# Loading and transposing q and k by head pair in a fused attention and maxout-FFN kernel

## The chip, the cores and the metric

The kernel runs on one core of one Trainium2 chip. The metric is the device time of one execution in microseconds, as the median of five runs. The core's engines go by the names of the profile: PE multiplies matrices (PEld loads its weights), DVE and ACT do elementwise work, POOL and SP mostly issue DMAs here.

## The reference

Attention with a relative-position bias over 8 batches, 8 heads, 576 positions and 64 channels, and then a feed-forward network with the largest of three products as its gate:

```python
scores = scale * np.matmul(q, k.transpose(0, 1, 3, 2)) + bias      # q, k, v: (8, 8, 576, 64), float32
attn = np.exp(scores - np.max(scores, axis=-1, keepdims=True))
attn = attn / (np.sum(attn, axis=-1, keepdims=True) + 1e-09)
attn_out = np.matmul(attn, v)
x = attn_out.transpose(0, 2, 1, 3).reshape(B * S, H * D)           # 4608 tokens of 512
h = np.maximum(np.maximum(x @ w1, x @ w2), x @ w3)                 # d_ff = 768
out = h @ w_out
```

The bias depends on the distance of the two positions only, by 32 buckets.

## The kernel before

**Steps.** The two heads of a pair share the 128 partitions, so the work goes in steps (b, hp): batch b from 0 to 7, head pair hp from 0 to 3. A step multiplies kT by qT into PSUM (`sc`, and `sct` and `scq` for the last 64 positions, the tail), ACT takes the exponential into bf16 (`e`, `el`; line 808), DVE multiplies a band around the diagonal by the bias (line 788), and a later step multiplies with v (`a`) and divides (`x_sb`). The FFN of an earlier chunk of 512 tokens is woven into the steps: `ps` and `psp` are its gates, `pso` and some `psp` its output. PE's instructions are in an order written out by hand (`keep_in_program_order`), so one late operand holds all of PE.

**Where q and k come from.** `load_qk` loads, on POOL's queue, for each of four blocks of 128 positions all eight heads of q, then of k, into tiles `q_sb` and `k_sb` of shape [128, KT, H, D] (line 189), and casts from float32 to bf16 on the way; the tails go to `qtail` and `ktail` (lines 170 and 192). From batch 2 on, `transposes(b)` turns them on SP's queue by DMA, one instruction for a block of positions with all four head pairs, ten in a batch (line 719), into `qT` and `kT` of shape [128, HP, positions]. Batch 1 takes another way: its q and k come in a packed layout into space of `xT`, `spread_packed` copies a head pair into `q_sb` and `k_sb` on DVE (line 236; the first pair on POOL), and PE transposes it. Step (1, hp) has the copies for pair hp + 1 ahead of its FFN portion.

**Order of the loads.** POOL's queue holds, one behind the other: the first weights, the packed batch 1, v of batch 1, `moe_w3`; then q and k of batch 2, all of it; then in step (1, 2) v of batch 2 (lines 161 and 180), the output weights `wo_bf` (line 1065) and q and k of batch 3; and in step (b, 2) v of batch b + 1 and q and k of batch b + 2. `go_behind` makes some of these wait for transposes: `load_v` for a named kT transpose of the same batch, `load_last_weights` and the next q and k for the last one of main blocks. From batch 5 on (`PACED`) a load also waits for the one four places ahead (`DEEP`). The weights load whole (line 1046).

**SP's queue.** It holds the q and k transposes, the transposes of finished attention rows `x_sb` into `xT` (lines 954 and 1002, five in a batch, which the FFN gates read), and the stores of outputs (lines 450 and 564). It works in order: what waits at its head holds the rest.

**Buffers.** q and k tiles, `qT` and `kT`, `x_sb` and v have two each, output rows five. In step (3, 0) the scores run in another order (`keys_first`), with both halves of the queries for the first two key blocks ahead of the others.

Of the kernel before, what the change touches and what calls it, by code (L numbers as in the profile page):

```python
# [39 lines left out]
def kernel(  # L40
# [12 lines left out]
    nc = tc.nc  # L53
# [8 lines left out]
    QM = 2 * QS  # L62
    KT = 4
    ROWS = (4, 0)
    PACED, DEEP = 5, 4
    FCH = d_ff // P
    DCH = d_model // P
    NTOK = B * S
# [73 lines left out]
    def main_part(src, b):  # L142
        return src[b, :, 0 : KT * P, :].rearrange("h (t p) d -> p t h d", p=P)

    def tail_part(src, b, h0, h1, par):
        return src[b, h0 + par : h1 : 2, KT * P : S, :].rearrange("h p d -> p h d")

    in_flight = []

    def in_turn(b, load):  # L150
        load = inorder(load)
        if b >= PACED:
            if len(in_flight) >= DEEP:
                go_behind([load], in_flight[-DEEP])
            in_flight.append(load)
        return load

    def load_main(src, b, h0, h1, dst, t0=0, t1=KT):
        x = main_part(src, b)
        return [  # L160
            in_turn(b, nc.gpsimd.dma_start(out=dst[:, t, h0:h1, :], in_=x[:, t, h0:h1, :])) for t in range(t0, t1)  # L161
        ]
# [5 lines left out]
    def load_q_tail(b):  # L168
        dst = qtail[b % 2][0 : S - KT * P].rearrange("p g (h d) -> p (g h) d", h=2)
        return in_turn(b, nc.gpsimd.dma_start(out=dst, in_=q[b, :, KT * P : S, :].rearrange("h p d -> p h d")))  # L170

    def k_diag(b, par, h0, h1):
        return diag(ktail[b % 2], par, h0, h1)
# [7 lines left out]
            for par in range(2)  # L181
        ]

    def load_qk(b, behind=None):

        loads = []
        for t in range(KT):
            for src, dst in zip((q, k), batch[b]):
                loads.append(in_turn(b, nc.gpsimd.dma_start(out=dst[:, t], in_=main_part(src, b)[:, t])))  # L189
        loads.append(load_q_tail(b))  # L190
        for par in range(2):
            load = nc.gpsimd.dma_start(out=k_diag(b, par, 0, H), in_=tail_part(k, b, 0, H, par))
            loads.append(in_turn(b, load))
        go_behind(loads, behind)

    def go_behind(loads, behind):

        for load in loads if behind else ():
            tc.add_manual_dep(
                load.ins, behind.ins.name,  # L200
                mybir.DependencyInfo(mybir.DependencyClass.Sync, mybir.DependencyReason.DATA),
                reason="these loads go behind the transposes in line",
            )

    def load_v(b, h0, h1, behind=None):
        loads = load_main(v, b, h0, h1, vx[b % 2][:, :, :, 0:D]) + load_tail(v, b, h0, h1, v_diag)
        go_behind(loads, behind)
        return loads[-1]

# [23 lines left out]
        for dst, src in zip(batch[1], (q_1, k_1)):  # L235
            inorder(eng.tensor_copy(dst[:, :, h, :], src[:, h].rearrange("p h t d -> p t h d")))  # L236

    def load_tiles():
        q_sb = loads.tile([P, KT, H, D], BF16, tag="q_sb", name="q_sb")
        k_sb = loads.tile([P, KT, H, D], BF16, tag="k_sb", name="k_sb")  # L240
        return q_sb, k_sb

    batch = [None] * B
    batch[0] = load_tiles()
# [464 lines left out]
    def transposes(b):  # L709

        made = qk_tiles()
        qk.append(made)

        def one(j, t):
            n = P if t < KT or j else S - KT * P
            src = batch[b][j][:, t].rearrange("p h d -> p (h d)") if t < KT else (
                (qtail, ktail)[j][b % 2][0:n].rearrange("p h c -> p (h c)")
            )
            turned_qk[b, j, t] = inorder(nc.sync.dma_start_transpose(out=made[j][:, :, P * t : P * t + n], in_=src))  # L719

        for t in range(KT + 1):
            one(0, t)
            one(1, t)
            yield

    def qk_tiles():
        return [qkt.tile([P, HP, n], BF16, tag=x, name=x) for x, n in (("qT", S), ("kT", (KT + 1) * P))]
# [174 lines left out]
            out=last_tile, in0=last_tile, in1=hank[:, 2 * hp : 2 * hp + 2, P - 64 : P][:, :, ::-1], op=ALU.mult,  # L902
        ))

    divided, turned_qk = {}, {}

    def attend(b, hp, e4, el, half):

# [134 lines left out]

    def load_w(i):
        src = (moe_w1, moe_w2, moe_w3)[i].rearrange("(c p) f -> p c f", p=P)
        in_turn(0, nc.gpsimd.dma_start(out=w_bf[i][:], in_=src))

    load_w(0)
    batch[1] = load_tiles()
# [11 lines left out]
        load_v(1, 0, H)  # L1061
        load_w(2)

    def load_last_weights(behind):
        load = in_turn(0, nc.gpsimd.dma_start(out=wo_bf[:], in_=moe_w_out.rearrange("(c p) m -> p c m", p=P)))
        go_behind([load], behind)

    def bands(hp):
        times_band_pair(hp, first_e[hp], 0, 0)
# [42 lines left out]
    for hp in range(HP):  # L1112
        qT, kT = (x[:, hp, :] for x in qk[0])
        if begun:
            e4, el = begun.pop()
            more_transposes(hp + 1)
            scores(qT, kT, e4, 1, 2)
        else:
            e4, el = e_tiles()
            visit(qT, kT, e4, [(1, 0), (1, 2)], (lambda: more_transposes(hp + 1)) if hp + 1 < HP else None)  # L1120

        def keys():
            left_keys(hp, qT, kT, el, QS, S)

        def queries():
            left_queries(hp, qT, kT, el)

        def late_bands(hp=hp, e4=e4):
            times_band(hp, e4, 1, QS, QM, inorder)
            times_band_pair(hp, e4, 2, QS)  # L1130

        if hp == 0:
            keys()
        if hp == 1:
            x_transposes(0, 0)
        quotients = next_late()
        if hp < 2:
            if hp == 0:
                make_bandt()
            quotients()  # L1140
            if hp == 0:
                bands(2)
            else:
                behind.pop()()
                keys()
            queries()
            if hp == 1:
                x_transposes(1, 0)
            else:
                begun.append(e_tiles())  # L1150
                scores(*(x[:, 1, :] for x in qk[0]), begun[0][0], 1, 0)
            quotients = next_late()
            quotients()
            if hp == 0:
                bands(3)
            behind.append(lambda late_bands=late_bands, hp=hp, el=el: (late_bands(), products(hp, el)))
        else:
            if behind:
                behind.pop()()
            if hp == 3:  # L1160
                quotients()
                add_ffn(0, QS)
                fill(8)
            keys()
            if hp == 2:
                quotients()
            queries()
            late_bands()
            if hp == 2:
                x_transposes(2, 0)  # L1170
                x_transposes(3, 0)
            else:
                batch[2] = load_tiles()
                load_qk(2)
                x_transposes(0, 1)
                fill(8, lambda: second_transposes(qk[1], 0))
            products(hp, el)
        late.append(lambda hp=hp, e4=e4, el=el: attend(0, hp, e4, el, 1))

    turned = [lambda hp=hp: x_transposes(hp, 1) for hp in range(1, HP)]  # L1180
    for b, hp in [(b, hp) for b in range(1, B) for hp in range(HP)]:
# [15 lines left out]

        if tiled:
            run, after = stages.pop(0)
        keys_first = (b, hp) == (3, 0)  # L1200
        order = [(0, 0), (1, 0), (0, 2), (1, 2)] if keys_first else [(0, 0), (0, 2), (1, 0), (1, 2)]
        if rows:
            lead = not begun
            begun.clear()
# [6 lines left out]
            for c, tt in order[:2]:  # L1211
                scores(qT, kT, e4, c, tt)
        store_outputs()
        if b == 1:
            if hp == 0:
                crossbar = transposes(2)
            next(crossbar, None)
        elif hp and b + 1 < B:
            if hp == 1:
                crossbar = transposes(b + 1)  # L1220
            for _ in range((KT + 1, 2, KT + 1)[min(b, 4) - 2]):
                next(crossbar, None)
        early()
        if turned:
            turned.pop(0)()
# [4 lines left out]
        quotients()  # L1230
        if rows:
            times_band(hp, e4, 1, 0, QM, inorder)
        if b == 1 and hp + 1 < HP:
            spread_packed(hp + 1, nc.vector)
        if (b, hp) == (1, 1):
            add_ffn(QS, QS)

# [64 lines left out]
        else:  # L1302
            late_keys = (b, hp) == (2, 0)
            fill(8 if (b, hp) == (2, 1) else rate, (lambda: None) if late_keys else keys, *([lambda: None] if together else []))
            if not late_keys:
                times_bandt(hp, el)

# [5 lines left out]

            visit(qT, kT, e4, order[2:], None if together else beside_scores, el=el if together else None)
        store_outputs()
        if b == 1 or hp in (1, 2) and b + 1 < B:
            for _ in range(2 if b > 1 else 1):
                next(crossbar, None)
        early()
        if turned:  # L1320
            turned.pop(0)()
# [6 lines left out]
        if hp == 1 and b > 1:  # L1328
            pending.extend((n, [fn]) for n, fn in rest)
            rest.clear()  # L1330
            made, tail = ffn((b - 1) * CH, CH, False, [(b + (i + 2) // HP, (i + 2) % HP) >= ROWS for i in range(HP)])
        if hp == 2 and b + 1 < B:
            load_v(b + 1, 0, H, turned_qk[b + 1, 1, 1 if b < 3 else 2 if b == 3 else KT - 1])
            if b == 1:
                load_last_weights(turned_qk[2, 1, KT - 1])
                batch[3] = load_tiles()
                load_qk(3, turned_qk[2, 1, KT - 1])
        if hp == 2 and 1 < b < B - 2:
            batch[b + 2] = load_tiles()
            load_qk(b + 2, turned_qk[b + 1, 1, KT - 1])  # L1340

        def queries():
            times_band(hp, e4, 3, 0, QM, inorder)
# [70 lines left out]
```

## Time and profile before

| | |
|---|---|
| device time, median of 5 runs | 310.24 us (308.88 to 312.71) |
| the profiled execution: device time, span | 310.34 us, 308.6 us |
| PE, PEld | 297.1 us (96%), 181.9 us (59%) |
| DVE, ACT, POOL | 207.1 us (67%), 202.0 us (65%), 110.5 us (36%) |
| granted PE clock | 1.0 throughout |
| DMA packets | 163950, of which 153784 are under 512 B |
| HBM read, written | 35.39 MB, 9.45 MB |

The span runs from the first to the last instruction of the program; the device time holds 1.74 us more. Busy times are unions over an engine's instructions. In the lines of a view, "<-" in brackets names what ended the idle time ahead of an instruction, and an issue on POOL or SP is the time that the queue took to hand a transfer over, not the time to its landing.

### The profile page before, as it was taken

To read this page: it belongs to the slowest core of one execution; us is meant where nothing else is said; L and a number is where in the kernel's file an instruction comes from. 1 tells how busy PE (TensorE), PEld (TensorE's weight loads), DVE (VectorE), ACT (ScalarE), POOL (GpSimd) and SP (SyncE) were. 2 spreads that over 40 slices of the span, in tenths; PEclk is the share of its full clock that TensorE was granted. 3 is DMA by queue.
4 is the path that set the end of the run, shared out by engine and by line. 5 is a ranking of instruction groups with operands and counts; after the bars stand their busy time and mean duration, and the time that the engine had idled before them with its cause. 6 is when DMAs were issued, how large, how long until landed. Compare 5 with 4: busy or idle time off the path is not lost.

```text
span 308.6 us, 10546 instructions
## 1 busy us (share of the span) xinstructions
PE 297.1 (96%) x4547; PEld 181.9 (59%) x4547; DVE 207.1 (67%) x471; ACT 202.0 (65%) x273; POOL 110.5 (36%) x147
## 2 busy tenths in 40 slices
PE   7889989989999999999999999999999999999995
PEld 2367867765555655657666766666667654444442
DVE  7497878766776767666777677766777665553552
ACT  3999979976777777758777777777777730222211
POOL 8978650962096106630555145434100000000000
PEclk9999999999999999999999999999999999999999
DMA  9999999999999999999999979997922113202003
GB/s 158 191 199 198 181 165 143 95 166 142 165 135 225 135 199 144 130 135 155 173 106 159 163 138 161 126 174 165 135 53 107 37 19 94 102 0 104 34 0 136
DMA packets 163950, 40.48 MB, mean 131 GB/s; under 512 B 153784, under 2 KB 159424, under 8 KB 163904
## 3 DMA queue, kind: packets, MB, share of 16 engines
q0 software_dynamic: 103840, 16.66, 85.0%
q1 hardware_dynamic: 58304, 22.69, 42.1%
q8 instruction: 35, 0.57, 0.8%
q10 hardware_dynamic: 1760, 0.47, 0.7%
q14 instruction: 11, 0.09, 0.1%
HBM read 35.39 MB, written 9.45 MB: 145 GB/s over the span
## 4 chain that ended last, share of the span: by engine, by line
PE 84%; DMA 5%; ACT 5%; SPq 3%; issue 1%; DVE 1%; ACTq 0%; POOL 0%
PE psp L108 34%; PE ps L108 17%; PE a L108 12%; PE sc L108 8%; PE pso L108 6%; ACT e L808 4%; SPq L719 3%; DMA wo_bf<-in_moe_w_out_dram 3%; PE sct L108 2%; PE scq L108 1%; PE warm L108 1%; DMA qT<-qtail 1%; DMA out_dram<-osb 1%; PE tp L112 1%; PE xp L112 0%
## 5 line engine op out<-in xcount | busy, mean ns | idle before, releaser
L808 ACT ACTIVATE e<-sc 128x1024 bf16<-128x1024 f32 x128 | 128.6, 1026 | 31.6 <-PE sc L108 30.3
L108 PEld LDWEIGHTS <-w_bf 64*128 64x128 bf16 (+1 forms) x1088 | 73.6, 95 | 57.2 <-issue 2.7
L108 PE MATMUL psp<-xT,w_bf 64*128 64x512 bf16 x736 | 91.4, 376 | 0.7 <-issue 0.7
L788 DVE TENSOR_TENSOR e<-e,hank 128x512 bf16<-128x512 bf16 (+2 forms) x120 | 56.4, 475 | 17.6 <-ACT e L808 17.2
L108 PE MATMUL ps<-xT,w_bf 128*128 128x512 bf16 (+1 forms) x352 | 65.1, 335 | 0.8 <-DVE q_sb L236 0.8
L108 PE MATMUL sc<-qT,kT 64*128 64x256 bf16 (+1 forms) x384 | 47.7, 306 | 2.1 <-ACT e L808 1.0
L108 PEld LDWEIGHTS <-kT 64*128 64x128 bf16 (+1 forms) x736 | 30.5, 94 | 26.7 <-issue 9.5
L108 PE MATMUL a<-vx,e 64*128 64x65 bf16 (+1 forms) x1536 | 44.6, 191 | 0.0
L161 POOL DMA_DIRECT2D vx<-in_v_dram x28 | 24.6, 894 | 55.7 <-DMA kT<-k_sb 32.2
L108 PEld LDWEIGHTS <-e 64*128 64x128 bf16 (+1 forms) x1536 | 40.7, 95 | 3.8
L108 PEld LDWEIGHTS <-hT 64*128 64x128 bf16 (+1 forms) x444 | 27.3, 95 | 20.1 <-issue 1.4
L108 PE MATMUL a<-vt,el 64*128 64x65 bf16 (+1 forms) x240 | 30.8, 201 | 0.2 <-DVE m L496 0.2
L406 ACT ACTIVATE m<-ps 128x512 bf16<-128x512 f32 x14 | 8.4, 597 | 34.3 <-PE ps L108 34.3
L108 PEld LDWEIGHTS <-el 64*128 64x128 bf16 (+1 forms) x624 | 26.0, 95 | 7.8 <-issue 5.2
L808 ACT ACTIVATE el<-sct 128x576 bf16<-128x576 f32 (+2 forms) x36 | 21.7, 606 | 13.3 <-PE sct L108 12.1
L108 PE MATMUL psp<-wo_bf,hT 64*128 64x256 bf16 (+1 forms) x336 | 29.7, 307 | 0.0
L189 POOL DMA_DIRECT2D k_sb<-in_k_dram x24 | 21.5, 895 | 11.1 <-DMA k_sb<-in_k_dram 6.3
L189 POOL DMA_DIRECT2D q_sb<-in_q_dram x24 | 21.5, 898 | 9.3 <-DMA q_sb<-in_q_dram 5.7
L108 PE MATMUL pso<-wo_bf,hT 128*128 128x512 bf16 (+2 forms) x108 | 23.2, 367 | 0.8 <-DMA wo_bf<-in_moe_w_out_dram 0.8
L808 ACT ACTIVATE el<-scq 128x512 bf16<-128x512 f32 (+1 forms) x38 | 19.5, 530 | 2.8 <-PE scq L108 2.7
L415 DVE TENSOR_TENSOR m<-ps,m 128x512 bf16<-128x512 f32 x14 | 9.7, 692 | 17.0 <-PE ps L108 17.0
L536 DVE TENSOR_TENSOR hT<-psp,m 128x1024 bf16<-128x1024 f32 (+1 forms) x16 | 15.0, 956 | 7.4 <-PE psp L108 7.4
(83 smaller groups left out, 291.8 us busy)
## 6 DMA issues: line engine op xcount, KB each, us to landing
out_dram<-osb SPq DMA_DIRECT2D x35, 256.0 KB, 3.9
vx<-in_v_dram POOLq DMA_DIRECT2D x28, 128.0 KB, 6.6
q_sb<-in_q_dram POOLq DMA_DIRECT2D x26, 128.0 KB, 7.4
k_sb<-in_k_dram POOLq DMA_DIRECT2D x24, 128.0 KB, 7.9
w_bf<-in_moe_w_dram POOLq DMA_DIRECT2D x3, 768.0 KB, 9.3
xT<-in_k_dram SPq DMA_DIRECT2D x6, 128.0 KB, 4.5
hank<-w_dr SPq DMA_DIRECT2D x2, 384.0 KB, 5.4
wo_bf<-in_moe_w_out_dram POOLq DMA_DIRECT2D x1, 768.0 KB, 9.8
```

What stands on the lines that cost most here:

```text
L108: made = inorder(nc.tensor.matmul(*args, **kw))
L112: inorder(nc.tensor.transpose(*args))
L161: in_turn(b, nc.gpsimd.dma_start(out=dst[:, t, h0:h1, :], in_=x[:, t, h0:h1, :])) for t in range(t0, t1)
L189: loads.append(in_turn(b, nc.gpsimd.dma_start(out=dst[:, t], in_=main_part(src, b)[:, t])))
L406: nc.scalar.activation(out=st[fb]["m0"][:], in_=ps0, func=ACTF.Copy)
L415: inorder(nc.vector.tensor_tensor(out=m[:], in0=ps1, in1=st[fb]["m0"][:], op=ALU.max))
L536: inorder(nc.vector.tensor_tensor(out=out_[:, i : i + n], in0=ps2()[:, i : i + n], in1=m[0][:, i : i + n], op=ALU.max,))
L719: turned_qk[b, j, t] = inorder(nc.sync.dma_start_transpose(out=made[j][:, :, P * t : P * t + n], in_=src))
L788: put(nc.vector.tensor_tensor(out=e4[:, t, :, lo:hi], in0=e4[:, t, :, lo:hi], in1=hank[:, 2 * hp : 2 * hp + 2, c0:c1][:, :, ::-1], op=ALU. ...
L808: made = nc.scalar.activation(out=out_, in_=in_, func=ACTF.Exp, scale=inv_sqrt_d)
```

## The change

From batch 2 on q and k are loaded by head: `load_pair(b, g)` issues four loads for head pair g (q and k, even and odd head), each with all four blocks of positions, into tiles of shape [128, HP, KT, 2, D]. A transpose takes one head pair with its four blocks (line 725 of the changed file), another the tails (line 732); there are ten in a batch as before. `begin_qk` loads pair 0, the tails and pair 1; `end_qk` loads pairs 2 and 3, and stands behind v of the same batch and, for batch 2, the output weights. The transposes stand in SP's order at places written out by step and half step. The loads wait for no transposes any more. From step (1, 1) on each load, v included, waits for the sixth one ahead of it. `moe_w2` and `moe_w3` load in two pieces, the first 256 columns and the other 512. The copies of `spread_packed` come behind the FFN portion of their step, and `keys_first` is gone.

```diff
-    PACED, DEEP = 5, 4
+    DEEP = 6
...
-        if b >= PACED:
-            if len(in_flight) >= DEEP:
+        if b > 1:
+            if len(in_flight) >= DEEP and paced:
                 go_behind([load], in_flight[-DEEP])
             in_flight.append(load)
...
-    def load_qk(b, behind=None):
...
-        for t in range(KT):
-            for src, dst in zip((q, k), batch[b]):
-                loads.append(in_turn(b, nc.gpsimd.dma_start(out=dst[:, t], in_=main_part(src, b)[:, t])))
...
-        go_behind(loads, behind)
+    def load_pair(b, g):
+        for src, dst in zip((q, k), batch[b]):
+            for par in range(2):
+                part = main_part(src, b)[:, :, 2 * g + par, :]
+                in_turn(b, nc.gpsimd.dma_start(out=dst[:, g, :, par, :], in_=part))
...
+    def begin_qk(b):
+        batch[b] = load_tiles(True)
+        load_pair(b, 0)
+        load_left(b)
+        load_pair(b, 1)
+
+    def end_qk(b):
+        for g in range(2, HP):
+            load_pair(b, g)
...
+        def pair(g):
+            for j in range(2):
+                inorder(nc.sync.dma_start_transpose(
+                    out=made[j][:, g, 0 : KT * P].rearrange("p (t n) -> p t n", t=KT),
+                    in_=batch[b][j][:, g].rearrange("p t h d -> p (t h d)"),
+                ))
...
+        return [lambda: pair(0), left] + [lambda g=g: pair(g) for g in range(1, HP)]
...
-        in_turn(0, nc.gpsimd.dma_start(out=w_bf[i][:], in_=src))
+        for f0, f1 in ((0, QS), (QS, d_ff)) if i else ((0, d_ff),):
+            in_turn(0, nc.gpsimd.dma_start(out=w_bf[i][:, :, f0:f1], in_=src[:, :, f0:f1]))
...
+    places = {2: ((1, 1, 0), (1, 1, 1), (1, 2, 0), (1, 3, 1), (2, 1, 0)), 3: ((2, 2, 0), (2, 2, 1), (2, 3, 0), (3, 0, 0), (3, 0, 1))}
+    for n in range(4, B):
+        places[n] = tuple((n - 1, hp, half) for hp, half in ((1, 0), (1, 1), (2, 0), (2, 1), (3, 0)))
...
-        if hp == 2 and b + 1 < B:
-            load_v(b + 1, 0, H, turned_qk[b + 1, 1, 1 if b < 3 else 2 if b == 3 else KT - 1])
+        if hp == 1 and b + 1 < B:
+            paced.append(b)
+            load_v(b + 1, 0, H)
             if b == 1:
-                load_last_weights(turned_qk[2, 1, KT - 1])
-                batch[3] = load_tiles()
-                load_qk(3, turned_qk[2, 1, KT - 1])
-        if hp == 2 and 1 < b < B - 2:
-            batch[b + 2] = load_tiles()
-            load_qk(b + 2, turned_qk[b + 1, 1, KT - 1])
+                load_last_weights()
+            end_qk(b + 1)
+        if hp == (2 if b == 1 else 1) and b + 2 < B:
+            begin_qk(b + 2)
```

More of the change, by code (lines that the diff above doesn't have):

```diff
@@ L146, in tail_part @@
         return src[b, h0 + par : h1 : 2, KT * P : S, :].rearrange("h p d -> p h d")
-    in_flight = []
+    in_flight, paced = [], []
     def in_turn(b, load):
         load = inorder(load)
-        if b >= PACED:
-            if len(in_flight) >= DEEP:
+        if b > 1:
+            if len(in_flight) >= DEEP and paced:
                 go_behind([load], in_flight[-DEEP])
@@ L182, in load_tail, with load_left @@
         ]
-    def load_qk(b, behind=None):
-        loads = []
-        for t in range(KT):
-            for src, dst in zip((q, k), batch[b]):
-                loads.append(in_turn(b, nc.gpsimd.dma_start(out=dst[:, t], in_=main_part(src, b)[:, t])))
[L190 to L193, printed above, removed]
-        go_behind(loads, behind)
+    def load_pair(b, g):
[3 more added lines that the diff above has]
+                in_turn(b, nc.gpsimd.dma_start(out=dst[:, g, :, par, :], in_=part))
+    def load_left(b):
+        load_q_tail(b)
+        load_tail(k, b, 0, H, k_diag)
+    def begin_qk(b):
[6 more added lines that the diff above has]
+            load_pair(b, g)
     def go_behind(loads, behind):
@@ L203, in go_behind, with load_v @@
             )
[L205 to L208, printed above, removed]
+    def load_v(b, h0, h1):
+        load_main(v, b, h0, h1, vx[b % 2][:, :, :, 0:D])
+        load_tail(v, b, h0, h1, v_diag)
     xT = const.tile([P, DCH, NTOK], BF16, name="xT")
@@ L236, in spread_packed, with load_tiles @@
             inorder(eng.tensor_copy(dst[:, :, h, :], src[:, h].rearrange("p h t d -> p t h d")))
[L238 to L241, printed above, removed]
+    def load_tiles(by_pair=False):
+        shape = [P, HP, KT, 2, D] if by_pair else [P, KT, H, D]
+        return [loads.tile(shape, BF16, tag=x, name=x) for x in ("q_sb", "k_sb")]
     batch = [None] * B
@@ L712, in transposes, with left @@
         qk.append(made)
[L714 to L724, printed above, removed]
+        def pair(g):
[4 more added lines that the diff above has]
+                ))
+        def left():
+            for j, n in enumerate((S - KT * P, P)):
+                inorder(nc.sync.dma_start_transpose(
+                    out=made[j][:, :, KT * P : KT * P + n],
+                    in_=(qtail, ktail)[j][b % 2][0:n].rearrange("p h c -> p (h c)"),
+                ))
+        return [lambda: pair(0), left] + [lambda g=g: pair(g) for g in range(1, HP)]
     def qk_tiles():
@@ L903, in times_band_left @@
         ))
-    divided, turned_qk = {}, {}
+    divided = {}
     def attend(b, hp, e4, el, half):
@@ L1062, in load_second, with load_last_weights @@
         load_w(2)
-    def load_last_weights(behind):
-        load = in_turn(0, nc.gpsimd.dma_start(out=wo_bf[:], in_=moe_w_out.rearrange("(c p) m -> p c m", p=P)))
-        go_behind([load], behind)
+    def load_last_weights():
+        in_turn(0, nc.gpsimd.dma_start(out=wo_bf[:], in_=moe_w_out.rearrange("(c p) m -> p c m", p=P)))
     def bands(hp):
@@ L1172 @@
             else:
-                batch[2] = load_tiles()
-                load_qk(2)
+                begin_qk(2)
                 x_transposes(0, 1)
@@ L1178, with turn_ahead @@
         late.append(lambda hp=hp, e4=e4, el=el: attend(0, hp, e4, el, 1))
+    turns = {n: [] for n in range(2, B)}
+    places = {2: ((1, 1, 0), (1, 1, 1), (1, 2, 0), (1, 3, 1), (2, 1, 0)), 3: ((2, 2, 0), (2, 2, 1), (2, 3, 0), (3, 0, 0), (3, 0, 1))}
+    for n in range(4, B):
+        places[n] = tuple((n - 1, hp, half) for hp, half in ((1, 0), (1, 1), (2, 0), (2, 1), (3, 0)))
+    def turn_ahead(*place):
+        for n, order in places.items():
+            if place == order[0]:
+                turns[n] = transposes(n)
+            if place in order:
+                turns[n].pop(0)()
     turned = [lambda hp=hp: x_transposes(hp, 1) for hp in range(1, HP)]
@@ L1199 @@
             run, after = stages.pop(0)
-        keys_first = (b, hp) == (3, 0)
-        order = [(0, 0), (1, 0), (0, 2), (1, 2)] if keys_first else [(0, 0), (0, 2), (1, 0), (1, 2)]
+        order = [(0, 0), (0, 2), (1, 0), (1, 2)]
         if rows:
@@ L1213 @@
         store_outputs()
[L1214 to L1222, printed above, removed]
+        turn_ahead(b, hp, 0)
         early()
@@ L1232 @@
             times_band(hp, e4, 1, 0, QM, inorder)
-        if b == 1 and hp + 1 < HP:
-            spread_packed(hp + 1, nc.vector)
         if (b, hp) == (1, 1):
@@ L1304 @@
             fill(8 if (b, hp) == (2, 1) else rate, (lambda: None) if late_keys else keys, *([lambda: None] if together else []))
+            if b == 1 and hp + 1 < HP:
+                spread_packed(hp + 1, nc.vector)
             if not late_keys:
@@ L1315 @@
         store_outputs()
-        if b == 1 or hp in (1, 2) and b + 1 < B:
-            for _ in range(2 if b > 1 else 1):
-                next(crossbar, None)
+        turn_ahead(b, hp, 1)
         early()
```

## The prediction

> **What bounds the kernel now.** I read the page first, then the busy time by stretches, then who waited for whom on PE, then the timeline around the longest waits. The page:
>
> ```profile
> span 308.6 us, 10546 instructions
> PE 297.1 (96%) x4547; PEld 181.9 (59%) x4547; DVE 207.1 (67%) x471; ACT 202.0 (65%) x273; POOL 110.5 (36%) x147
> ...
> q0 software_dynamic: 103840, 16.66, 85.0%
> q1 hardware_dynamic: 58304, 22.69, 42.1%
> ```
>
> PE is busy for all but 11.5 us; loads from POOL (q0) and transposes and stores from SP (q1) share 16 DMA engines that are seldom empty. Where the 11.5 us lie (columns: span and busy us of PE, PEld, DVE, ACT, POOL):
>
> ```profile
> 0.00:40.00 40.00, 35.31 (x484) 22.84 (x485) 29.48 (x108) 33.47 (x55) 33.40 (x51) 1.00 1.50 186
> 40.00:72.00 32.00, 29.87 (x458) 22.04 (x457) 23.26 (x64) 26.34 (x42) 15.50 (x20) 1.00 1.83 138
> 72.00:250.00 178.00, 177.02 (x3329) 111.68 (x3328) 125.70 (x257) 131.75 (x160) 61.60 (x77) 1.00 1.50 140
> 250.00:304.00 54.00, 54.00 (x275) 24.83 (x272) 27.79 (x43) 10.15 (x17) 0.00 (x0) 1.00 0.18 57
> ```
>
> 4.7 us are lost before 40 us, in batch 0, and 3.7 us after 304 us, in the last store; the change touches neither. Its part holds 2.13 us (40 to 72) and 0.98 us (72 to 250) of idle PE: 3.1 us, 1.0% of the time, is all that any better supply of q, k, v and weights can win while PE's instructions stay the same. They do: as many matmuls of the same shapes, only the scores of step (3, 0) in another order. What PE waited for between 40 and 250 us (total us, times, longest):
>
> ```profile
> PE pso L108 <- DMA wo_bf<-in_moe_w_out_dram: 0.8, 1, 0.8
> PE ps L108 <- DVE q_sb L236: 0.8, 1, 0.8
> PE psp L108 <- issue: 0.7, 2, 0.4
> PE sc L108 <- DVE qT L125: 0.3, 1, 0.3
> ```
>
> And the pieces of the timeline behind them:
>
> ```profile
> 41.06 0.77 PEld L108 LDWEIGHTS <-w_bf 128*128 128x128 bf16 x8 [1.07 <-DMA w_bf<-in_moe_w_dram]
> 41.07 1.05 PE L108 MATMUL ps<-xT,w_bf 128*128 128x256 bf16 x8 [0.77 <-DVE q_sb L236]
> ...
> 53.96 3.53 POOL L161 DMA_DIRECT2D vx<-in_v_dram  x4 [8.88 <-DMA kT<-k_sb]
> 57.44 1.30 POOL L180 DMA_DIRECT2D vt<-in_v_dram  x2
> 58.67 0.91 POOL L1065 DMA_DIRECT2D wo_bf<-in_moe_w_out_dram  x1
> ...
> 61.59 7.98 SPq L954 DMA_TRANSPOSE xT<-x_sb  x5
> ...
> 68.48 1.46 PE L108 MATMUL pso<-wo_bf,hT 128*128 128x512 bf16 x6 [0.83 <-DMA wo_bf<-in_moe_w_out_dram]
> ```
>
> The second line blames a DVE copy, but its weight load waited, to the same moment, for `moe_w3` to land: that is the cause. POOL stood 8.88 us behind a transpose of batch 2, so `wo_bf` was issued at 58.67, took 9.8 us, and PE waited.
>
> **The change part by part.** *Weights in pieces.* `moe_w3` was issued at 31.72 and landed at 41.06. Its first piece, a third of the bytes and all that the waiting matmuls read, is issued at the same place and lands ahead of the other two thirds. PE asks 0.77 us before 41.07, at 40.3; two thirds of the bytes after the earlier landings (v of batch 1, up to 37.8 us: 30.15, the second issue of L180, plus 7.6) leave the first piece at about 37.8 + 3.3 / 3 = 38.9. Gain 0.77 us; bounds 0 and 0.77. The price is two more issues on POOL at 0.785 us (the median of the three weight issues), beside waits of POOL for older loads (0.90 and 1.46 us at 31 to 34 us).
>
> *`wo_bf` earlier.* POOL's waits for transposes go. The eleven issues of `begin_qk(2)` start at 33.93 as the old ones did: eight half-size loads at 0.79 (the row of eight half-size v loads, 745 to 814 ns), 0.69 for `qtail`, 2 x 0.63 for `ktail`, with the 1.24 and 0.97 us that POOL waited there before: 33.93 + 6.3 + 1.95 + 2.2 = 44.4. Then v, 3.53 + 1.30, so `wo_bf` goes out at 49.2 instead of 58.67 and lands, with the same 9.8 us, at 59.0. PE asks at 67.6. Gain 0.83; cover 8.6 us, and without it the 0.83 are back.
>
> *Tails earlier.* The tails of batch 2 were transposed last (56.13) and a weight load waited 0.26 us for them at 63.58, PE idling 0.14 between 60 and 64; they now go second. Gain 0.14, bounds 0 and 0.26.
>
> *`spread_packed` later.* Six copies of 0.28 us stand behind an FFN maximum of 0.69. In step (1, 1) that was 42.15 to 42.84 and starts about 0.77 earlier, so the copies end near 42.7, PE's transposes ask at 43.62 - 0.77 = 42.85. In step (1, 2) they end near 50.7, PE asks at 50.79. That is tight: cost 0.1 us, bounds 0 and 3 x 0.57 = 1.7.
>
> *Half-size loads.* Per batch sixteen issues of 0.79 in place of eight of 0.89: 12.6 - 7.1 = 5.5 us more on POOL, 33 us over six batches, on an engine busy 61.6 of 178 us between 72 and 250. Bytes and rows are the same. Cost 0 on PE, hidden by nothing that PE needs within a step: pair 0 of batch 4 and later is turned three steps ahead of its use.
> [...]
>
> *Pacing and places.* With six in flight, the queue is never deeper than before. But SP now has the later pairs in its way, and here a new wait can appear. Pairs 2 and 3 of batch 2 are loaded behind `wo_bf`: eight issues from 50.1, the last of pair 2 at 52.4. The same tile's loads landed in 8.0 us (batch 2 before: 7.9 to 8.1) or 13.3 (batch 3 before, 12.6 to 13.8, beside the xT transposes), so pair 2 is in at 60.4 to 65.7. I take 61: no xT transpose is issued yet, but `wo_bf` is ahead. SP then turns it, 1.2 us for the last, until 62.3. Behind it on SP stand the five xT transposes of batch 1, which would be free at 61.59 - 0.9 = 60.7. The FFN gates of step (2, 2), first at 77.1 and now at 75.5, read four of them. The fourth leaves 3 x 1.3 us after the first, at 66.2, and lands in 8.2 to 9.2 us: 75.0. It just holds; cost 0, and at the late bound 65.7 + 1.2 + 3.9 + 9.2 = 80.0 it would be 4.5 us.
>
> *`keys_first` gone:* the order of the other steps, cost 0; bounds ±0.3, the wait for qT above.
>
> Sum: -0.77 - 0.83 - 0.14 + 0.1 = -1.6 us. Span 308.6 to 307.0; the profiled 310.34 to 308.7; the median of runs stands 0.10 below the profiled time, so **308.6 us**.
>
> **The rivals.** *Everything idle vanishes.* The two 0.7 us of "issue", the qT wait and the rest close too, 3.1 us: 307.1 us. For it: all of them fall where DMAs are dense. Against: "issue" is a wait for nothing that the profile shows, and the qT wait is a PE-DVE round trip in batch 1.
>
> *SP held up by the late pairs.* At the late bound PE loses 4.5 us at step (2, 2). The same queue order comes again with batch 3 (pair 2 at step (3, 0), ahead of xT of batch 2), where the loads landed in 9.8 to 15.2 us; taking half the stall there, the time is 310.2 - 1.6 + 4.5 + 2.2 = 315.3 us. For it: POOL's loads no longer leave the DMA engines to the transposes, and at 59 to 70 us mixing cost them 13 instead of 8 us. Against: v and `wo_bf` are out of the way earlier, and from step (4, 2) on the gates need only blocks that landed long before. It decides once pair 2 lands more than half a microsecond after 61, and passes 1% (4.7 us of stall against 1.6 of gain) when that is some 5 us late, or 3 us at both places.
>
> *The gains are given back.* Less of the same delay, or the copies of `spread_packed` at their bound: 310 us, no change.
>
> **How the numbers follow.** What a measurement can tell from no change is about 1%, 3.1 us, and the whole idle PE of the stretch is just that; so faster by over 1% needs the first rival and luck: 0.12. My forecast has 0.50 and its own range is 307.3 to 309.7; the gains given back have 0.14; both are within 1%, 0.64. The held-up SP queue has 0.24, since one late load there decides it. The range goes from the first rival, 307.0, into the held-up queue to 313.5.
>
> **What would show it.** Right: no wait of PE for `wo_bf` and of PEld for `w_bf` after 40 us; POOL without waits for kT; PE idle between 40 and 72 near 0.5 us; `wo_bf` issued near 49. Wrong: PE waiting for xT ahead of the first `psp` near 75, or SP's first xT transpose of batch 1 later than 63; a PE wait for q_sb copies; more PE idle than 1 us between 72 and 250. If PE's busy time itself changes, the whole argument is wrong.

## The result, and the profile after

| | before | changed |
|---|---|---|
| device time, median | 310.64 us | 309.47 us (307.15 to 312.92) |
| ratio to before, 95% interval | | 0.9958 [0.9945, 0.9970] |
| the profiled execution: device time, span | 310.34, 308.6 us | 307.93, 306.2 us |
| PE idle between 40 and 72 us, 72 and 250 us | 2.13, 0.98 us | 0.73, 0.31 us |

The ratio is a gain of 1.3 us in 310.6 (0.42%, interval 0.30 to 0.55%): less than the 1% that the prediction could hope to tell from no change, but clear of no change here. The before of this table was measured beside the changed kernel, so its median differs from the five runs shown at the start. The ratios here and below leave out the executions counted as a slow state, so they can differ from the quotient of the medians (here 0.9962; most of all in `e1_deep4` and `e2_deep8`, with five and four of twelve left out).

The page of the changed kernel, its first lines and its queues:

```profile
span 306.2 us, 10608 instructions
...
PE 296.7 (97%) x4547; PEld 181.7 (59%) x4547; DVE 208.4 (68%) x471; ACT 201.8 (66%) x273; POOL 141.3 (46%) x197
...
q0 software_dynamic: 105664, 16.66, 91.0%
q1 hardware_dynamic: 58304, 22.69, 38.7%
```

PE does the same 4547 matmuls in nearly the same time (296.7 us for 297.1). POOL has 50 instructions and 31 us more, and PE does not feel them. The bytes are the same. The loads of q, in the kernel before and then in the changed one (count, size of one, median us from issue to landing):

```profile
q_sb<-in_q_dram POOLq DMA_DIRECT2D x26, 128.0 KB, 7.4
```

```profile
q_sb<-in_q_dram POOLq DMA_DIRECT2D x50, 64.0 KB, 4.8
```

The busy time by stretches (span, then busy us of PE, PEld, DVE, ACT and POOL, the PE clock, DMA, GB/s):

```profile
40.00:72.00 32.00, 31.27 (x472) 22.82 (x470) 25.04 (x67) 27.18 (x43) 22.30 (x31) 1.00 1.92 142
72.00:250.00 178.00, 177.69 (x3355) 112.39 (x3352) 126.78 (x260) 130.98 (x159) 85.73 (x115) 1.00 1.51 139
```

The profiled span is 2.4 us shorter: 1.40 us of idle PE went between 40 and 72 us, 0.67 us between 72 and 250 us, and PE's busy time is 0.4 us shorter. This execution lies 1.5 us under the median of the changed kernel (307.93 for 309.47). All that PE still waited for in it between 30 and 250 us:

```profile
PE sc L108 <- DVE qT L125: 0.3, 1, 0.3
PE a L108 <- DVE m L505: 0.2, 1, 0.2
```

The waits for `wo_bf` and `w_bf` are gone, and so are the two of "issue". POOL and SP show how. POOL's issues from 48 us on, then SP's:

```profile
48.56 1.33 POOL L180 DMA_DIRECT2D vt<-in_v_dram  x2
49.79 0.93 POOL L1079 DMA_DIRECT2D wo_bf<-in_moe_w_out_dram  x1
...
62.10 1.19 SPq L725 DMA_TRANSPOSE qT<-q_sb  x1
63.39 1.21 SPq L725 DMA_TRANSPOSE kT<-k_sb  x1
64.76 6.96 SPq L967 DMA_TRANSPOSE xT<-x_sb  x5
```

`wo_bf` is issued 8.9 us sooner than before (49.79 for 58.67) and landed at 60.17; PE asks for it at 67.04. The first xT transpose of batch 1 is 3.2 us later than before (64.76 for 61.59) and nobody waits for it. The gates that read the xT transposes start at 75.70, without a wait:

```profile
75.70 1.03 PE L108 MATMUL psp<-xT,w_bf 64*128 64x512 bf16 x8
```

### The profile page after: what moved, and what is told of

It is laid out like the page before. It is cut to its first block, busy times and chain, and to the rows that moved or that the text cites. A ratio compares the mean times of both kernels' runs of the same rounds, so it can differ in the third digit from the quotient of the medians.

```text
span 306.2 us, 10608 instructions
## 1 busy us (share of the span) xinstructions
PE 296.7 (97%) x4547; PEld 181.7 (59%) x4547; DVE 208.4 (68%) x471; ACT 201.8 (66%) x273; POOL 141.3 (46%) x197
## 3 DMA queue, kind: packets, MB, share of 16 engines
q1 hardware_dynamic: 58304, 22.69, 38.7%
## 4 chain that ended last, share of the span: by engine, by line
PE 87%; ACT 7%; DVE 2%; issue 1%; DMA 1%; ACTq 0%; DVEq 0%
PE psp L108 34%; PE ps L108 18%; PE a L108 14%; PE sc L108 9%; PE pso L108 6%; ACT e L821 5%; PE sct L108 2%; PE scq L108 1%; PE warm L108 1%; ACT el L821 1%; DMA out_dram<-osb 1%; PE tp L112 1%; DVE qT L125 1%; PE xp L112 0%; DVE hT L421 0%
## 5 line engine op out<-in xcount | busy, mean ns | idle before, releaser
L189 POOL DMA_DIRECT2D k_sb<-in_k_dram x48 | 36.0, 759 | 17.3 <-DMA vx<-in_v_dram 10.0
L189 POOL DMA_DIRECT2D q_sb<-in_q_dram x48 | 36.2, 760 | 15.5 <-DMA vx<-in_v_dram 8.5
```

Source lines behind the costliest of these rows:

```text
L189: in_turn(b, nc.gpsimd.dma_start(out=dst[:, g, :, par, :], in_=part))
```

## The experiments

Each kernel was timed in five rounds beside the kernel before; all are ratios to that kernel. Two questions: is the gain the two weight waits alone (theories A and H of the expectations below), and does the rest of the change (the order by head pair, the place of the later pairs, the pacing) carry it or only accompany it?

| run | edit | median, us | ratio [95%] |
|---|---|---|---|
| a0_after | the changed kernel again | 309.33 | 0.9965 [0.9940, 0.9991] |
| b1_pieces | before, weights in pieces | 310.62 | 1.0019 [0.9989, 1.0050] |
| b2_ungated | before, v and `wo_bf` behind no transposes | 317.30 | 1.0220 [1.0179, 1.0260] |
| b3_both | both of these | 317.86 | 1.0281 [1.0225, 1.0337] |
| a1_whole | changed, weights whole | 309.42 | 0.9974 [0.9953, 0.9995] |
| a3_late | changed, `wo_bf` loaded twice | 317.21 | 1.0205 [1.0158, 1.0252] |
| c1_wo_later | changed, pair 2 ahead of `wo_bf` | 309.78 | 0.9975 [0.9947, 1.0002] |
| c3_pairs_first | changed, pairs 2 and 3 ahead of v | 309.02 | 0.9955 [0.9926, 0.9984] |
| e1_deep4 | changed, four loads in flight | 314.28 | 1.0079 [1.0038, 1.0119] |
| e2_deep8 | changed, eight | 312.17 | 1.0003 [0.9958, 1.0048] |
| a6_paced_early | changed, no pacing from batch 4 on | 311.52 | 1.0013 [0.9974, 1.0052] |
| a2_unpaced | changed, no pacing | 312.19 | 1.0055 [1.0023, 1.0088] |

### The two weight waits alone

The changed kernel again:

> The changed kernel again, as the measure for the runs beside it. Both theories expect what it showed: about 1.3 us under the kernel before (ratio 0.996), PE idle near 0.7 us between 40 and 72 us and near 0.3 us from 72 to 250.

The time came again, but its profiled execution had a wait that the first did not:

```profile
PE sc L108 <- DMA kT<-k_sb: 1.9, 1, 1.9
```

It ends at 81.09, in step (2, 3): the kT transpose of pair 3 of batch 2 stands on SP behind the five xT transposes, went out at 74.07 and took 6.97 us to land, beside the loads of v of batch 3 (5.3 us from 73.14 in the first profile, and no wait). So the order of SP's queue is close to PE's path in some executions. PE idled 0.80 us between 40 and 72 us, near the 0.73 of the first profile, but 2.93 us between 72 and 250 us, where the first had 0.31: the part won at the weights came again, what lies behind it varies.

Weights in pieces, in the kernel before:

```diff
-        in_turn(0, nc.gpsimd.dma_start(out=w_bf[i][:], in_=src))
+        for f0, f1 in ((0, QS), (QS, d_ff)) if i else ((0, d_ff),):
+            in_turn(0, nc.gpsimd.dma_start(out=w_bf[i][:, :, f0:f1], in_=src[:, :, f0:f1]))
```

> The kernel before with one part of the change: the second and third gate weights load in two pieces. Theory A (the gain is the two waits for weights): the wait of 0.77 us near 41 us goes, 0.8 us less, ratio 0.9975; the wait of 0.83 us for the output weights stays. Theory B (the gain is the relief of the DMA engines by the new order and pacing): the wait moves elsewhere in batch 1, ratio 1.000.

No gain: 1.0019, and theory A's 0.9975 lies outside the interval. PE's waits between 30 and 250 us:

```profile
PE pso L108 <- DMA wo_bf<-in_moe_w_out_dram: 1.9, 1, 1.9
PE xp L112 <- DVE hT L412: 0.8, 1, 0.8
PE sc L108 <- DVE qT L125: 0.3, 1, 0.3
PE psp L108 <- issue: 0.3, 1, 0.3
```

The wait at 41 us is gone and the one for `wo_bf` grew from 0.83 to 1.94 us. Of the 1.11 us more, 0.26 are PE's coming earlier (67.39 for 67.65) and 0.85 are `wo_bf` itself, which went out 0.45 us later and let PE go on at 69.33 instead of 68.48. PE was not earlier by the full 0.77 us because this execution had lost 0.81 us already, ahead of the weights:

```profile
35.37 0.33 PE L112 MATMUL xp<-ident,x_sb 128*128 128x128 bf16 x3 [0.81 <-DVE hT L412]
```

No other profile has that wait. With it or without it PE stops at `wo_bf`, whose load stands behind v, and v behind a kT transpose (8.98 us of waiting on POOL). A PE that is early waits the longer there (by the 0.26 us of `b1_pieces`), so a gain ahead of it is given back.

The other wait, in the kernel before:

```diff
-                load_last_weights(turned_qk[2, 1, KT - 1])
+                load_last_weights(None)
...  (and the first load_v, of batch 2, without its wait)
```

> The kernel before with another part: v of batch 2 and the output weights do not wait for transposes of batch 2 any more, all else as before. Theory A: the output weights go out near 50 us instead of 58.7 and land near 60, the wait of 0.83 us at 68.5 goes, ratio 0.9973. Theory B: these loads now run beside the ten transposes of batch 2, whose block-by-block order needs all of them before step (2, 0) at 58.5 us; they land later than 57 us and PE waits there for qT or kT, 1 to 4 us, ratio 1.000 to 1.010.

> The kernel before with both of these parts and none of the order by head pair. Theory A: both waits go, 1.6 us less, ratio 0.995, as much as the whole change. Theory B: the wait at step (2, 0) for qT or kT eats it, ratio 0.998 to 1.008, and the order by head pair is what makes the earlier loads pay.

Both kernels are slower by 2.2 and 2.8%, more than theory B expected. The longest wait of `b2_ungated`, and PE's clock around it (the number ahead of the DMA share):

```profile
PE sc L108 <- DMA kT<-k_sb: 5.6, 1, 5.6
```

```profile
59.00:65.00 6.00, 0.65 (x7) 0.27 (x6) 2.14 (x6) 1.38 (x2) 0.00 (x0) 0.73 1.32 176
65.00:68.00 3.00, 2.73 (x27) 2.12 (x28) 0.61 (x2) 1.02 (x1) 2.14 (x3) 0.50 0.32 35
68.00:72.00 4.00, 4.00 (x63) 3.11 (x62) 1.69 (x4) 2.69 (x5) 4.00 (x6) 0.92 2.18 122
```

The fourth kT transpose of batch 2 was issued at 53.52 in both kernels, but beside the loads of v and `wo_bf` it took 11.7 us to land where it took 3.6. Before, then `b2_ungated`:

```profile
DMA to landing us min/median/max: 3.6/3.6/3.6
```

```profile
DMA to landing us min/median/max: 11.7/11.7/11.7
```

In the order by blocks of positions the first step of a batch needs all four of its kT transposes, so PE lost 5.6 us at step (2, 0). In `b3_both` the same wait is 6.4 us. That ends theory A: in the old order, as it stands, the loads could not be let go earlier. In the new order that step reads pair 0 and the tails alone; in the changed kernel pair 0's kT landed at 48.97, some nine microseconds before PE asks.

The changed kernel differs from `b3_both` in the order by pair and in the limit of six loads in flight. `a2_unpaced` below has the order without the limit and no wait at step (2, 0), so the order is enough there. The old order with the limit was not run; whether the limit alone would have done is open.

Weights whole, in the changed kernel:

```diff
-        for f0, f1 in ((0, QS), (QS, d_ff)) if i else ((0, d_ff),):
-            in_turn(0, nc.gpsimd.dma_start(out=w_bf[i][:, :, f0:f1], in_=src[:, :, f0:f1]))
+        in_turn(0, nc.gpsimd.dma_start(out=w_bf[i][:], in_=src))
```

> The changed kernel with moe_w2 and moe_w3 loaded whole, as before; all else as changed. The prediction's term: the first piece of moe_w3 was worth 0.77 us. Theory H (the later deadlines now have room, so what comes back stays): PE's weight load waits again for w_bf near 41, some 0.8 us; two issues fewer on POOL save nothing that PE needs; ratio to the kernel before 0.9985, that is 0.25% above the changed kernel. Rival I (the later deadlines absorb it, as they did when the pieces were put into the kernel before, where 0.8 us at 41 moved to wo_bf): the same 0.996.

```profile
PE ps L108 <- DMA w_bf<-in_moe_w_dram: 1.5, 1, 1.5
```

The wait came back, at 41.87, and twice as long as before the change. PE's other waits up to 250 us are the two of the changed kernel, so in this execution nothing later absorbed it. (The profiled span is 1.0 us above that of the changed kernel, but two executions of the changed kernel itself differ by 2.0 us, 306.2 and 308.2.) The ratio, 0.9974, lies between theory H (0.9985) and rival I (0.996), and its interval holds both: the profile speaks for H, the times do not decide it.

### The place of the later pairs

```diff
+            load_pair(b + 1, 2)
             if b == 1:
                 load_last_weights()
-            end_qk(b + 1)
+            load_pair(b + 1, 3)
```

> The changed kernel with pair 2 of batch 2 loaded ahead of wo_bf, pair 3 behind it. Theory C: wo_bf was 6.9 us ahead of its use, so it can stand some 3 us behind; pair 2 lands near 59 instead of 62, SP's pair-2 and xT transposes and pair 3's go out 2 to 3 us earlier, and the wait of 1.9 us for kT of pair 3 seen in one execution of the changed kernel has gone. Ratio to the kernel before 0.993 to 0.996. Rival F: nothing there was on PE's path in most executions, so the time is that of the changed kernel, 0.996, or wo_bf lands after 67 and costs 0.5 us or more, 0.998.

```diff
+            if b == 1:
+                end_qk(b + 1)
             load_v(b + 1, 0, H)
             if b == 1:
                 load_last_weights()
-            end_qk(b + 1)
+            else:
+                end_qk(b + 1)
```

> The changed kernel with pairs 2 and 3 of batch 2 loaded ahead of v of batch 2 and wo_bf, not behind. Theory C (the later pairs may wait, v and wo_bf may not): wo_bf is issued some 6 us later, near 56, lands at 67 to 69, PE waits up to 2 us for it or for v at 62 to 68; ratio to the kernel before 0.998 to 1.003. Rival G (the place of the later pairs makes no difference; the order by pair alone did it): no wait of PE, SP's queue runs earlier, ratio 0.994 to 0.996.

Neither differs from the changed kernel within the intervals; F and G hold. In `c3_pairs_first` `wo_bf` went out at 57.70 and PE waited only 0.23 us for it. SP's first xT transpose went out at 60.84 instead of 64.76, and that bought nothing. The xT transposes issued between 60 and 72 us, in the changed kernel and in `c3_pairs_first`:

```profile
DMA to landing us min/median/max: 3.7/4.5/5.2
```

```profile
DMA to landing us min/median/max: 8.8/9.1/10.2
```

The fourth landed at 73.44 in the first and at 75.28 in the second: here an earlier issue lands later. Over the profiles these transposes go with `wo_bf`. Where it had landed 3 us and more before the first of them (the changed kernel twice, `a2_unpaced`, `a3_late`, `a6_paced_early`, `e1_deep4`, `e2_deep8`) they took 3.7 to 6.8 us; where it had gone out only 2 to 5 us before (the kernel before, `b1_pieces`, `c1_wo_later`, `c3_pairs_first`) 7.8 to 10.2 us; where it landed about then (`b2_ungated`, `b3_both`) 5.5 to 8.5 us. That the 16 DMA engines, on which the page counts all the queues, are the cause is argued from this; no run shows it by itself.

### An SP queue held up

The changed kernel with the output weights loaded twice, one load behind the other:

```diff
             if b == 1:
                 load_last_weights()
+                load_last_weights()
             end_qk(b + 1)
```

> The changed kernel with the load of wo_bf issued twice, so that pairs 2 and 3 of batch 2 have 0.79 MB more ahead of them. It prices the prediction's rival of an SP queue held up. By the prediction's chain: pair 2 lands at 66 to 67 instead of 62, SP's first xT transpose goes out near 69, the fourth lands near 78 where PE asks at 75.7: PE waits 2 to 3 us at step (2, 2), pair 3's kT comes as much later: ratio to the kernel before 1.003 to 1.006. Theory E (SP's queue has more room than the prediction gave it, because the transposes land in half of the 8.2 to 9.2 us taken): the fourth xT lands before 76.5, PE waits under 1 us, ratio 0.996 to 0.999.

```profile
PE pso L108 <- DMA wo_bf<-in_moe_w_out_dram: 2.6, 1, 2.6
PE psp L108 <- DMA xT<-x_sb: 2.1, 1, 2.1
PE sc L108 <- DVE qT L125: 0.4, 1, 0.4
PE sc L108 <- DMA kT<-k_sb: 0.3, 1, 0.3
```

The ratio, 1.0205, is above the 1.003 to 1.006 expected. The edit delayed more than intended: the second load went out at 61.53 and PE had to wait for that one too, so the run prices two things. With `wo_bf` in at 69.77 PE waited 2.65 us; with pair 2 in at 71.4 it waited 2.12 us for xT at step (2, 2) and 0.31 for kT. The mechanism of the prediction's rival is real and has its place there. The profiled span is 6.8 us above that of the changed kernel (313.0 for 306.2): the four waits are 5.4 us, 0.3 of which the changed kernel has too, and PE's clock was at 0.50 from 70.5 to 74.0 us, right behind the first wait, which is 1.7 us of work more (an estimate: half of 3.4 us). One microsecond of that stretch (the clock is the third number from the end):

```profile
71.00:72.00 1.00, 1.00 (x12) 0.21 (x10) 0.10 (x1) 0.00 (x0) 1.00 (x3) 0.50 0.46 29
```

This execution was the shortest of six.

### How many loads in flight

`a2_unpaced` leaves the limit out, `a6_paced_early` keeps it for batches 2 and 3, `e1_deep4` and `e2_deep8` change the one number:

```diff
-            if len(in_flight) >= DEEP and paced:
+            if len(in_flight) >= DEEP and paced and b < 0:      # a2_unpaced; a6_paced_early has b < 4
...
-    DEEP = 6
+    DEEP = 4                                                    # e1_deep4; e2_deep8 has 8
```

> The changed kernel without the pacing of six loads in flight; nothing else differs, and the order of instructions on every engine is the same. Theory C (the gain of 1.3 us rests on the order by head pair, and the pacing keeps the DMA engines free enough for SP's transposes): POOL issues batch 3 right behind batch 2, loads land in 8 to 13 us instead of 4.5, SP's xT transposes of batch 1 in 8 to 9 us instead of 4.5, the fourth near 77.5 where PE asks at 75.7. PE waits some 2 us for xT or for kT of pair 3; ratio to the kernel before about 1.002. Rival D (the same bytes have to pass in any order, the pacing does nothing for PE): no new wait of PE, ratio 0.996 as the changed kernel.

> The changed kernel with the pacing of six kept for batches 2 and 3 and taken away from batch 4 on. It tells where the 1% of the unpaced kernel was lost. Theory J (lost behind 100 us, where three times as many loads stand in the queues, as PE stalls of 0.3 to 1.9 us in which PE waits for nothing that the profile shows): the loss stays, ratio 1.002 to 1.007, and the profile shows such stalls between 100 and 200 us. Rival L (lost between 58 and 85 us, at the transposes of batches 1 and 2): the loss goes, ratio 0.996.

> The changed kernel with four loads in flight in place of six. Theory J (without any pacing the time rose by 1%, so the loads that stand in the DMA queues are what delays the rest, PE's own instruction loads among them; fewer in flight delay less): no wait of 'issue' on PE, transposes land in 4 to 6 us, ratio 0.993 to 0.996. Rival K (six is enough, four starves the loads): POOL waits longer between loads, pair 2 or pair 3 lands 1 to 3 us later, PE waits for kT near 79 to 81 or at a later step; ratio 0.998 to 1.005.

> The changed kernel with eight loads in flight in place of six. So far: four 1.008, six 0.996 to 0.9965, no limit 1.0055. Theory M (two costs cross: too few in flight makes the tails' loads, and with them SP's queue, late; too many keeps PE's instruction loads waiting in the DMA engines, for PE stalls of 0.3 to 1.9 us behind 120 us): eight lies on the flat between them or a little up the second slope, 0.996 to 1.001, with none or one such stall. Rival N (six was not the best place, the loads still starve at six): 0.990 to 0.994, with fewer waits of POOL and no PE wait.

The pacing matters: the ratio is 1.008 with four in flight, 0.996 with six and 1.0055 with no limit. Eight gave 1.0003, and its interval overlaps that of six; theory N (0.990 to 0.994) is outside it, and theory M's range holds, but with one pause more than it allowed and a kT wait of 1.80 us.

With four in flight theory J's 0.993 to 0.996 failed. The loads starve, rival K, though not where it was placed. PE waited for the transposed tails of later batches:

```profile
PE sct L108 <- DMA kT<-ktail: 1.8, 2, 1.5
```

These 1.8 us belong to the shortest of twelve executions (310.40 us, median 314.28). Where the others lost more is not shown.

Without a limit the time rose, against rival D, but theory C's place was wrong: the xT transposes still landed in 5.2 to 6.1 us, and there is no wait near 75 us. What PE lost lay later, and no tile explains it. PE in `a2_unpaced`:

```profile
131.10 0.31 PE L108 MATMUL a<-vx,el 64*128 64x65 bf16 x8
133.16 1.04 PE L108 MATMUL psp<-xT,w_bf 64*128 64x512 bf16 x8 [1.75 <-DVE e L801]
```

The named DVE instruction ended at 131.42, 1.74 us before PE went on. The trace points to instruction loads. The queue q8, which the page calls "instruction", brings 16384 bytes about every 6 us (14 times between 100 and 190 us); the page does not say for which engine, and that they are PE's is the author's reading. Here one load landed at 125.1 and the next began only at 130.72 and landed at 131.92, and PE went on 1.24 us behind it. The DMA view of `a2_unpaced` from 130.60 to 131.95 has it:

```profile
q0 software_dynamic: 899, 0.11, 148.4%
q1 hardware_dynamic: 408, 0.10, 70.2%
q8 instruction: 1, 0.02, 5.6%
```

The fourteen profiles hold, between 100 and 200 us, fifteen pauses of PE of 0.2 us and more that end without an operand that has just come: twelve are called "issue", three name a DVE instruction that ended 0.5 us or more before. Every one ends 1.2 to 1.7 us behind the landing of an instruction load. By chance about one in twelve would, with a half-microsecond window in 6 us. So the tie between these pauses and instruction loads is shown by the traces; that PE stood for want of these instructions is the reading that fits all fifteen, and no run makes the instruction loads late by themselves.

That deeper load queues cause the pauses is not shown. For it: `a2_unpaced` has 1.75 and 0.28 us of them, `a6_paced_early` 1.11, 0.21 and 0.90, `e2_deep8` 0.78 and 0.91, the first profile of the changed kernel none, `a0_after` 0.44, `e1_deep4` none. Against it: `c1_wo_later`, with six in flight, has 0.46, 1.86 and 0.28 us, the largest sum of all:

```profile
157.84 0.39 PE L108 MATMUL sc<-qT,kT 64*128 64x512 bf16 x2 [1.86 <-issue]
```

The kernel before and its three variants have one pause each, of 0.28 to 0.88 us. `a6_paced_early` (1.0013) decides between J and L by its profile alone: the pauses lie where J has them, but its interval reaches from 0.9974 to 1.0052.

No variant beats the changed kernel: `c3_pairs_first` at 0.9955 cannot be told from its 0.9958.

## Why the prediction was right, and where not

The forecast was 308.6 us, a gain of 1.6; measured were 309.47 us and a gain of 1.3. Of the 0.9 us between the times, 0.4 is the higher median of the kernel before in the later comparison. The rest is probably waits that come in some executions only, such as the 1.93 us for kT and the 0.44 us pause of `a0_after`; how often they come is not shown. With them `a0_after` idled 2.93 us between 72 and 250 us, which meets a sign that the prediction named for "wrong" (more than 1 us), while the first profile, with 0.31 us, does not.

- *PE is the bound, and 3.1 us the most to win.* Right: PE busy 296.7 us for 297.1. The profiled execution took 2.1 of the 3.1 us.
- *`moe_w3` in pieces, 0.77 us.* Right in mechanism and time: first piece issued at 32.37 and in at 39.26 (38.9 predicted), wait gone. Its worth holds only together with the earlier `wo_bf`: by itself it gave nothing (`b1_pieces`), a dependence that the sum, which adds its terms, did not state.
- *`wo_bf` earlier, 0.83 us.* Right: issued 49.79 (49.2), in at 60.17 (59.0), cover 6.9 us (8.6). `a3_late` shows the deadline: in at 69.77, PE waits 2.65 us.
- *Tails, 0.14 us.* Right: PE is busy for all 4.00 us between 60 and 64 us, 3.86 before.
- *`spread_packed` later, 0.1 us, bounds to 1.7.* It cost nothing that shows: the one wait for qT copies is 0.31 us at 52.29, as before. A term mis-sized by 0.1 us.
- *Half-size loads, 0.* Right. POOL's busy time went from 110.5 to 141.3 us, near the 33 us more that were said, and the q loads landed in a median of 4.8 us, with 7.4 before. That eight more issues a batch cost PE nothing was the author's estimate; half-size loads ran side by side already in the kernel before, where the eight of v were issued between 9.2 and 14.5 us and landed in 3.9 to 6.1 us each, and in the changed kernel neither of PE's two waits between 30 and 250 us ends on a load.
- *Pacing and places, 0.* The result was right, the step was wrong twice, and by luck the errors cancelled. The limit of six was taken to cost nothing, but POOL stood 2.9 us in it behind loads of v (1.23, 1.07 and 0.60 us), and the last load of pair 2 went out at 55.87, not 52.4. Pair 2 came in at 62.6 at the latest, not 61, and SP's first xT at 64.76, which was one of the signs named for "wrong" (later than 63). But the xT transposes landed in 3.7 to 5.2 us, not in the 8.2 to 9.2 taken from before, where v and `wo_bf` ran beside them; here these had landed. The limit of six is not what made them quick: without it they took 5.2 to 6.1 us (`a2_unpaced`). The fourth was in at 73.44, not 75.0, and PE asks at 75.70.
- *The rival of a held-up SP queue, 0.24.* Its point of decision, half a microsecond behind 61, was too early: with 2.26 us of room left at pair 2 in at 62.6, PE would wait from about 64.9 on (an estimate, 62.6 + 2.26). `a3_late` confirms mechanism and place. It has a second place that the prediction did not see: kT of pair 3, behind the xT transposes, 1.93 us in `a0_after` and 1.80 in `e2_deep8`.
- *"Issue" stays.* Read as a wait for nothing that the profile shows, and left in the forecast. In these traces it is a real cost, 0.21 to 1.86 us in each of the fifteen pauses above, tied to instruction loads (each ends 1.2 to 1.7 us behind one), and it varies from one execution to the next: none and 0.44 us in the two profiles of the changed kernel. That both pauses were gone in the first profile of the changed kernel can therefore not be counted as won by the change.

## What to carry to other kernels

A gain ahead of a transfer can be given back at that transfer (in `b1_pieces` the 0.77 us at 41 us went and the wait for `wo_bf` grew from 0.83 to 1.94 us); add up single waits only after asking which one is next. Order operands by who reads them first (here by head pair), and only then let loads go early: the same early loads cost over 2% in the old order and paid 0.4% in the new one, with six in flight. Loads, transposes, stores and instruction loads are all counted on the same 16 DMA engines (91.0% for q0, 38.7% for q1, 0.8% for q8 in the changed kernel), and the ratio was 1.008 with four loads in flight, 0.996 with six and 1.0055 without a limit; so how many may be in flight is a setting to measure from both sides.

## What the hardware showed beyond expectation

- A DMA transpose landed in 3.6 us in the kernel before and in 11.7 us in `b2_ungated`, the same instruction issued at the same time (53.52), there beside the loads of v and `wo_bf`; the xT transposes took a median of 4.5 us in the changed kernel and 9.1 us in `c3_pairs_first`.
- Instruction loads of 16384 bytes about every 6 us (q8, 14 between 100 and 190 us), with pauses of PE of up to 1.86 us (`c1_wo_later`) that end 1.2 to 1.7 us behind one of them.
- Two PE stalls cost more than themselves: with 5.6 us of waiting in `b2_ungated` (59.7 to 65.27) the granted clock was 0.50 for about 6.8 us in all, from 61.8 to 68.6 (3.4 of them with PE working again), and behind 2.65 us in `a3_late` for 3.4 us (70.5 to 74.0). Waits of 1.93 us (`a0_after`) and 1.94 us (`b1_pieces`) left it at 1.00.
